# Clearing the zero tile first, modelling the last loads later, ranking the sink-row copies of V behind ready work, and a new order for TensorE

## The chip, the cores and the metric

The kernel runs on one core of a Trainium2 chip. The metric is the device time of one execution in microseconds (us), given as the median of the runs shown. The core's engines are named as in the profile: PE is TensorE (matrix products and transpositions), DVE is VectorE, ACT is ScalarE, POOL is GpSimd and SP is SyncE. POOL and SP also issue DMA transfers.

## The reference

Windowed attention with sinks over q, k and v of shape (4 batches, 8 heads, 768 rows, 64 wide), followed by a feed-forward block without a nonlinearity other than a product:

```python
scores = scale * np.matmul(q, k.transpose(0, 1, 3, 2))
keep = is_sink | in_window          # 4 sink keys, window of 128
a = softmax(np.where(keep, scores, -1e9))
x = np.matmul(a, v)                 # heads side by side: (3072, 512)
h = (x @ w1) * (x @ w2) @ w3        # 512 -> 1024 -> 1024
out = h @ w_out                     # 1024 -> 512
```

Inputs and output are float32; the kernel computes in bfloat16 with float32 sums.

## The kernel before

The work is cut into 350 TensorE tasks. Each task is a generator (a function with `yield` between its stages), and its later stages run on ACT, DVE or SP. The names in this text are the names of the tasks in the tables of the code:

- `("t3", i, h)`, function `fold_w3` (L525): four 128x128 transpositions of row block i of w3, half h, then a copy on DVE (L534). `("fm", i, h)`, function `fold_mm` (L548): two products of such a transposed block with w_out. Together they fold w3 and w_out into one matrix, w3o, which ACT copies out (L563, L566). The products of i = 4 to 7 keep one PSUM buffer from h = 0 to h = 3.
- `("tpk", b, kb)` (L244): eight transpositions of block kb of k and q of batch b, four of k first, then four of q, then one copy on DVE (L251). For batches 2 and 3 SP transposes by DMA instead (L256), one transfer for k and one for q of each block.
- `("sc", b, r, t)`: the score products of one unit, the exponential on ACT (L332, L385, L406), the mask product on DVE. `("ss", b, t)` is the same for the sink keys. `("av", ...)`: the products with V (L364, L435, L472) and the normalisation on DVE (a reciprocal and a product). `("xt", ...)` transposes the result on PE and copies it on ACT (L453, L492); for batches 1 to 3 SP does it by DMA (L499, `xd`).
- `("g", b, c, dt, half)`, function `gate` (L505): four products of the attention output with w1 (half 0, copied by ACT, L519) or w2 (half 1, multiplied by DVE, L516, into the tile `ab`). A gate has 256 columns in batches 0 and 1, and 320 (c = 0) or 448 (c = 1) in batches 2 and 3.
- `("p", b, m)`, function `project` (L569): eight products with w3o, a copy (L577), and the store to HBM (L582).
- `vo` (`own_values`, L272), for batches 2 and 3: DVE copies V rows into `vp` (L275), and then V's four sink rows into the blocks of `vN` that a unit reads (L278). `ko` (L259) copies keys into `kown` (L262 to L269).

PSUM has a pool of four buffers (`ps_mm`, for t3, tpk, av, xt, gates, projections, and fm of i = 4 to 7) and a pool of two (`ps_sc`, for scores and for fm of i = 0 to 3). A task takes the buffer that is oldest free, and so waits until ACT or DVE has emptied it.

The order is written by the program before it runs. `TURNS` (L827) is PE's list, task by task. `plan` (L903) walks through it with a table of durations and of arrival times of the loads (`landings`, L609, fills `arrive`), and gives ACT, DVE and SP their instructions in the order in which the model would start them. `LEAN` and `YIELD` are numbers that are added to a step's modelled start when two ready steps of one engine are compared: a higher one ranks the step later, a negative one earlier. Each engine executes its list strictly in this order, so an instruction that waits holds back everything behind it on its engine. Where the model sees a gap of over 0.5 us on PE in the first 40 us, `keep_busy` (L586) writes dummy products of a zero tile (`ksbd[1]`, the variable `idle`) into the list; their result, `pz`, is not read. How many there are follows from the modelled gap.

Loads go two ways. SP brings nine raw float32 blocks of w3 and w_out first (L181), and ACT and DVE cast them to bfloat16 (L539). SP's next instructions are eight little loads for `vc` (L225). When the fifth block is there, POOL starts its own loads, which convert on the way (L122 for k and q, L125 for V, L129 and L143 for weights), in the order of the list `order` (L165). With eight loads out, the next one waits for the oldest to land.

Of the kernel before, what the change touches and what calls it, by code (L numbers as in the profile page):

```python
# [21 lines left out]
def kernel(  # L22
# [13 lines left out]
    nc = tc.nc  # L36
# [68 lines left out]
    ksbd = [inp.tile([P, 648], BF16, name=f"ksbd_{b}") for b in range(2)]  # L105
# [59 lines left out]
    order = [("w3", 6, 8), ("qkv", 0, 0, 1), ("qkv", 0, 1, 2), ("w3", 5, 6), ("qkv", 0, 2, 3), ("qkv", 0, 3, 4),  # L165
# [23 lines left out]
    idle = ksbd[1][:, 0:512]  # L189
    nc.vector.memset(ident[:], 1.0)  # L190
    nc.vector.memset(maskt[:], 1.0)
    nc.vector.memset(vc[:], 0.0)
    for b in (1, 0):
        nc.vector.memset(ksbd[b][:], 0.0)  # L194
# [398 lines left out]
    arrive = {}  # L593
# [15 lines left out]
    def landings(RAW=2.0, POOL=3.0, DGE=1.3, RAMP=(0.75, 1.0)):  # L609
# [6 lines left out]
        while any(at[n] < len(q) for n, q in queues.items()):  # L616
# [11 lines left out]
            for n in busy:  # L628
                i = int(now - RAW) if now >= RAW else 0
                share = 1.0 if len(busy) == 1 else 0.5 if small not in "kqv" else 0.79 if n == "sp" else 0.13  # L630
                left[n][at[n]] -= 0.02 * share * (RAMP[i] if i < len(RAMP) else 1.0)
                if left[n][at[n]] <= 0.0:
                    lag, keys = queues[n][at[n]][2:]
                    for key in keys:
                        arrive[key] = now + lag + min(1.5, max(0.0, 0.25 * (now - 36.0))) + min(3.0, max(0.0, 0.1 * (now - 70.0)))
                    if n == "pool":
                        landed.append(now + lag)
                    at[n] += 1
# [158 lines left out]
    for b in range(B):  # L797
        for c, (t0, t1) in enumerate(CHUNKS[b]):
# [17 lines left out]
            for m in range(t0 // P, t1 // P):  # L816
# [10 lines left out]
    TURNS = [("t3", 0, 1), ("t3", 0, 0), ("t3", 2, 0), ("fm", 2, 0), ("t3", 4, 0), ("fm", 0, 0), ("t3", 2, 1), ("fm", 2, 1),  # L827
# [221 lines left out]
```

## Time and profile before

| what | us |
|---|---|
| median of 3 runs | 197.05 (196.99 to 197.65) |
| the profiled execution's own time | 196.85 |
| its span, first to last instruction | 195.1 |
| PE busy | 187.1 (96%) |
| DVE busy | 121.9 (62%) |
| ACT busy | 102.7 (53%) |
| POOL busy | 79.4 (41%) |

The profile comes from one execution. Its own time is 1.75 us longer than its span, which runs from the first to the last instruction. A row of the timeline has the start, the duration, the engine, the line of the code, the operation with output and input, and how many instructions were merged; in brackets stands how long the engine had been idle before and what ended that. Row names are without numbers, so `tp<-ident,w_sb` is a t3, `pz<-ksbd` a dummy, `ph` and `pw` are fm, `pg` a gate and `po` a projection. A group's row has the busy time and mean duration in ns, and after a second bar the idle time in front of it.

### The profile page before, as it was taken

Reading aid. Unit: us, or ns where it says so; the run is one execution under the profiler, and the core shown is the slowest. Engines: PE = TensorE matmul, PEld = TensorE weight load, DVE = VectorE, ACT = ScalarE, POOL = GpSimd, SP = SyncE. Lnnn points to the kernel's source line nnn. Section 1 sums busy time; section 2 is a strip of 40 time slices with the busy share of each in tenths; the row PEclk is TensorE's granted clock in tenths of the full one; section 3 lists DMA queues with packets and bytes.
Section 4 is the critical chain, followed back from the end, with each engine's and each line's share of the span. In section 5 each row is a group of like instructions: output and inputs, shape, how many; then the busy total and the mean of one; then the engine's idle time right before and its main releaser. Section 6 shows DMA issues by size and latency. Waiting matters only on the chain.

```text
span 195.1 us, 4747 instructions
## 1 busy us (share of the span) xinstructions
PE 187.1 (96%) x1880; PEld 123.7 (63%) x1880; DVE 121.9 (62%) x293; ACT 102.7 (53%) x172; POOL 79.4 (41%) x111
## 2 busy tenths in 40 slices
PE   3989999999999999999999999999899999999993
PEld 1444665898877776787986766665456665455542
DVE  4375689756789988778766686556567883124300
ACT  4051288753776768466446583365385653243322
POOL 5189977699999953532355343000000000000000
PEclk9999999999999999999999999999999999999999
DMA  6999999999999999999999999999930102420034
GB/s 218 370 388 174 169 160 199 194 161 154 157 152 182 188 128 125 156 186 192 116 184 151 127 200 148 216 187 131 208 72 0 35 16 79 133 108 0 0 105 168
DMA packets 110102, 29.43 MB, mean 151 GB/s; under 512 B 100736, under 2 KB 105984, under 8 KB 110080
## 3 DMA queue, kind: packets, MB, share of 16 engines
q0 software_dynamic: 81600, 12.59, 95.6%
q1 hardware_dynamic: 28336, 16.47, 40.2%
q8 instruction: 15, 0.25, 0.5%
q14 instruction: 7, 0.06, 0.1%
q10 hardware_dynamic: 144, 0.07, 0.1%
HBM read 29.90 MB, written 6.29 MB: 186 GB/s over the span
## 4 chain that ended last, share of the span: by engine, by line
PE 67%; DMA 28%; DVE 2%; issue 1%; POOL 0%; ACT 0%; POOLq 0%; DVEq 0%
PE pg L512 27%; DMA vN<-in_v_dram 17%; PE po L573 13%; DMA qN<-in_q_dram 10%; PE pw L559 4%; PE pz L590 3%; PE ph L559 3%; PE tp L249 3%; PE av L472 3%; PE sc L380 2%; PE tp L529 2%; PE av L435 1%; PE sc L402 1%; PE av L364 1%; PE sc L329 1%
## 5 line engine op out<-in xcount | busy, mean ns | idle before, releaser
L512 PE MATMUL pg<-xT,w_sb 128*128 128x256 bf16 (+2 forms) x640 | 92.0, 294 | 0.8 <-DVE ab L516 0.8
L512 PEld LDWEIGHTS <-w_sb 128*128 128x128 bf16 x640 | 59.8, 98 | 23.0 <-issue 1.9
L516 DVE TENSOR_TENSOR ab<-a_sb,pg 128x256 bf16<-128x256 f32 (+2 forms) x80 | 37.3, 472 | 32.7 <-PE pg L512 27.8
L519 ACT COPY a_sb<-pg 128x256 f32<-128x256 f32 (+2 forms) x80 | 32.8, 416 | 34.0 <-PE pg L512 28.9
L573 PE MATMUL po<-w3o,ab 128*128 128x512 bf16 (+2 forms) x208 | 44.4, 363 | 0.0
L573 PEld LDWEIGHTS <-ab 128*128 128x128 bf16 x208 | 19.3, 98 | 18.8 <-issue 0.2
L125 POOL DMA_DIRECT2D vN<-in_v_dram x26 | 23.5, 908 | 16.5 <-DMA kN<-in_k_dram 8.6
L577 ACT COPY w_sb<-po 128x512 f32<-128x512 f32 (+2 forms) x25 | 14.1, 564 | 28.0 <-PE po L573 27.8
L122 POOL DMA_DIRECT2D qN<-in_q_dram x24 | 21.7, 903 | 10.2 <-DMA vN<-in_v_dram 5.6
L332 ACT ACTIVATE ex<-sc 128x928 bf16<-128x928 f32 (+1 forms) x24 | 22.5, 972 | 4.5 <-PE sc L329 4.5
L122 POOL DMA_DIRECT2D kN<-in_k_dram x24 | 21.7, 906 | 7.2 <-DMA qN<-in_q_dram 3.2
L385 ACT ACTIVATE ex<-sc 128x1024 bf16<-128x1024 f32 (+1 forms) x16 | 15.1, 970 | 3.2 <-PE sc L380 3.0
L336 DVE TENSOR_TENSOR am<-ex,maskt 128x928 bf16<-128x928 bf16 (+1 forms) x24 | 15.3, 652 | 2.3 <-ACT ex L332 2.2
L371 DVE TENSOR_TENSOR xn<-av,rec 112x256 bf16<-112x256 f32 (+1 forms) x24 | 11.2, 468 | 0.8
L364 PEld LDWEIGHTS <-am 128*128 128x128 bf16 x208 | 8.9, 98 | 2.5
L590 PE MATMUL pz<-ksbd 128*128 128x512 bf16 x20 | 7.2, 521 | 3.2 <-DVE ksbd L194 3.2
L390 DVE TENSOR_TENSOR am<-ex,maskt 128x1024 bf16<-128x1024 bf16 (+1 forms) x16 | 10.0, 648 | 0.2 <-ACT ex L385 0.2
L251 DVE COPY kqT<-tp 128x1024 bf16<-128x1024 bf16 x12 | 8.3, 689 | 2.9 <-PE tp L249 2.8
L364 PE MATMUL av<-vN,am 128*128 128x65 bf16 x144 | 9.4, 193 | 0.0
L559 PE MATMUL ph<-wo_sb,kown 128*128 128x512 bf16 x32 | 9.1, 380 | 0.2
L534 DVE COPY kown<-tp 128x512 bf16<-128x512 bf16 x12 | 4.9, 420 | 6.7 <-PE tp L529 6.6
L406 ACT ACTIVATE ex<-sc 128x1024 bf16<-128x1024 f32 x7 | 7.1, 1029 | 3.7 <-PE sc L402 3.7
(85 smaller groups left out, 186.4 us busy)
## 6 DMA issues: line engine op xcount, KB each, us to landing
out_dram<-w_sb SPq DMA_DIRECT2D x20, 256.0 KB
vN<-in_v_dram POOLq DMA_DIRECT2D x26, 128.0 KB, 8.9
kN<-in_k_dram POOLq DMA_DIRECT2D x24, 128.0 KB, 8.0
qN<-in_q_dram POOLq DMA_DIRECT2D x24, 128.0 KB, 8.3
w_sb<-in_moe_w_dram POOLq DMA_DIRECT2D x9, 256.0 KB, 8.2
ab<-in_moe_w_dram SPq DMA_DIRECT2D x4, 512.0 KB
ab<-in_moe_w_out_dram SPq DMA_DIRECT2D x2, 512.0 KB
out_dram<-w_sb SPq DMA_DIRECT2D x7, 128.0 KB
```

Source lines behind the costliest of these rows:

```text
L122: nc.gpsimd.dma_start(out=heads(dst[b][:, kb, :]), in_=rows(src, b, kb * P, (kb + 1) * P))
L125: nc.gpsimd.dma_start(out=vN[b][:, s, :, 0:D], in_=rows(v, b, t0, t1))
L332: nc.scalar.activation(ex[:, :, 0:n], sc[:, :, 0:n], ACTF.Exp, scale=scale)
L336: nc.vector.tensor_mul(am[:, :, 0:n], ex[:, :, 0:n], maskt[:, mv:mv + 1, 0:n].to_broadcast([P, 2, n]))
L364: nc.tensor.matmul(o, lhs, rhs, start=(x == 0), stop=(x == len(todo) - 1), skip_group_check=True)
L385: nc.scalar.activation(ex[:, :, c0:], sc[:, :, c0:], ACTF.Exp, scale=scale)
L512: nc.tensor.matmul(pg[:], w_sb[:, kk, dt * P:(dt + 1) * P], xT[b][:, kk, tk], start=(kk == 0), stop=(kk == NP - 1))
L516: nc.vector.tensor_mul(ab[b][:, dt, tk], gate_a.pop((b, c, dt))[:], pg[:])
L519: nc.scalar.copy(a_sb[:], pg[:])
L559: nc.tensor.matmul(po, w3T[i][:, j, :], wo_sb[:, j, :], start=(j == 0), stop=(j == KFF - 1))
L573: nc.tensor.matmul(po[:], ab[b][:, kk, m * P:(m + 1) * P], w3o[:, kk, n0:n1], start=(kk == 0), stop=(kk == KFF - 1))
L577: (nc.vector.tensor_copy if n0 == DM // 2 else nc.scalar.copy)(o_sb, po[:])
```

## The change

Five things are changed.

1. In the program's head, the tile of zeros that the dummies read is the first that DVE clears. Before, it was the fourth (the identity, the masks and `vc` came first).
2. In POOL's list of loads, block 2 of batch 0 (k, q, v) goes ahead of row block 5 of w3.
3. In `landings`, loads that the model has landing after 112 us are taken to land up to 4.5 us later.
4. `YIELD` has an entry for `vo`, 0.8: a copy of V's rows ranks behind other work that would start up to 0.8 us after it.
5. `TURNS` and `LEAN` are replaced. The same 350 tasks stand in TURNS, in another order.

```diff
-    order = [("w3", 6, 8), ("qkv", 0, 0, 1), ("qkv", 0, 1, 2), ("w3", 5, 6), ("qkv", 0, 2, 3), ("qkv", 0, 3, 4),
+    order = [("w3", 6, 8), ("qkv", 0, 0, 1), ("qkv", 0, 1, 2), ("qkv", 0, 2, 3), ("w3", 5, 6), ("qkv", 0, 3, 4),
...
     idle = ksbd[1][:, 0:512]
+    nc.vector.memset(ksbd[1][:], 0.0)
     nc.vector.memset(ident[:], 1.0)
     nc.vector.memset(maskt[:], 1.0)
     nc.vector.memset(vc[:], 0.0)
-    for b in (1, 0):
-        nc.vector.memset(ksbd[b][:], 0.0)
+    nc.vector.memset(ksbd[0][:], 0.0)
...
-                        arrive[key] = now + lag + min(1.5, max(0.0, 0.25 * (now - 36.0))) + min(3.0, max(0.0, 0.1 * (now - 70.0)))
+                        arrive[key] = now + lag + min(1.5, max(0.0, 0.25 * (now - 36.0))) + min(3.0, max(0.0, 0.1 * (now - 70.0))) + min(4.5, max(0.0, 0.2 * (now - 112.0)))
...
-    TURNS = [("t3", 0, 1), ("t3", 0, 0), ("t3", 2, 0), ("fm", 2, 0), ("t3", 4, 0), ("fm", 0, 0), ("t3", 2, 1), ("fm", 2, 1),
+    TURNS = [("t3", 0, 0), ("t3", 4, 0), ("t3", 2, 0), ("fm", 0, 0), ("t3", 0, 1), ("fm", 4, 0), ("fm", 0, 1), ("t3", 4, 1),
...
-    LEAN = {(("t3", 2, 0), 1): -0.4, (("t3", 3, 0), 1): -1, (("sk", 0), 0): 0.4, (("xt", 0, 0, 1), 1): 1, (("sc", 0, 1, 2),
+    LEAN = {(("c", "wo", 2, 0), 0): 1, (("t3", 0, 1), 1): 1, (("t3", 5, 0), 1): -2.5, (("t3", 7, 0), 1): 1, (("tpk", 0, 2),
...
-    YIELD = {"g": 0.0, "av": 0.0, "sc": 0.4, "tdk": 1.5, "tdq": 1.5}
+    YIELD = {"vo": 0.8, "g": 0.0, "av": 0.0, "sc": 0.4, "tdk": 1.5, "tdq": 1.5}
```

What stands in the engines' lists now. On DVE at the start of the program, before (ksbd_1_112 is the zero tile; tp3_205 and tp3_210 are t3(0,1) and t3(0,0); tp3_225 is t3(2,0); ab_0_103 and ab_1_104 hold raw weights, the second cast is row block 2 of w3 and the third row block 4):

```order
L190 MEMSET ident_73 128x128
L191 MEMSET maskt_75 128x1536
L192 MEMSET vc_74 128x128
L194 MEMSET ksbd_1_112 128x324
L194 MEMSET ksbd_0_111 128x324
L539 CAST w3_sb_80<-ab_0_103 128x1024
L534 COPY kown_2_109<-tp3_205 128x512
L534 COPY kown_2_109<-tp3_210 128x512
L539 CAST w3_sb_80<-ab_0_103 128x1024
L534 COPY kown_3_110<-tp3_225 128x512
L539 CAST w3_sb_80<-ab_1_104 128x1024
```

The same place of the same engine in the changed kernel (tp3_205 is t3(0,0), tp3_227 is t3(4,0), tp3_232 is t3(2,0)):

```order
L190 MEMSET ksbd_1_112 128x324
L191 MEMSET ident_73 128x128
L192 MEMSET maskt_75 128x1536
L193 MEMSET vc_74 128x128
L194 MEMSET ksbd_0_111 128x324
L539 CAST w3_sb_80<-ab_0_103 128x1024
L534 COPY kown_2_109<-tp3_205 128x512
L539 CAST w3_sb_80<-ab_0_103 128x1024
L539 CAST w3_sb_80<-ab_1_104 128x1024
L534 COPY kN_1_88<-tp3_227 128x512
L534 COPY kown_3_110<-tp3_232 128x512
```

The zero tile has moved from the fourth place to the first, and the three casts of w3 have only one copy between them. PE's list begins with 12 dummies, t3(0,1), t3(0,0), 6 dummies, t3(2,0), 2 dummies before; now with 12 dummies, t3(0,0), 13 dummies, t3(4,0), t3(2,0), and no dummy after that.

On DVE late in the program, where the last V blocks of batch 3 are copied, before (vN_3_94 is V of batch 3; av_2530 and av_2560 are av(3,2,0) and av(3,3,0); pg_2550, pg_2589 and pg_2596 are the gates (2,1,0,1), (2,1,2,1) and (2,1,1,1)):

```order
L371 TENSOR_TENSOR xn_2495<-av_2530,rec_2547 128x3x128
L275 COPY vp_3_108<-vN_3_94 128x576
L278 COPY vN_3_94<-vN_3_94 4x1152
L516 TENSOR_TENSOR ab_2_105<-a_sb_2557,pg_2550 128x448
L269 COPY kown_3_110<-kqT_3_98 128x4x124 x2
L368 RECIPROCAL rec_2586<-av_2560 128x6
L371 TENSOR_TENSOR xn_2495<-av_2560,rec_2586 128x3x128
L516 TENSOR_TENSOR ab_2_105<-a_sb_2594,pg_2589 128x448
```

And there now (av_2538 and av_2567 are av(3,2,0) and av(3,3,0); pg_2560, pg_2588, pg_2604 and pg_2640 are the gates (2,1,0,1), (2,1,1,1), (2,1,2,1) and (2,1,3,1)):

```order
L371 TENSOR_TENSOR xn_2475<-av_2538,rec_2556 128x3x128
L516 TENSOR_TENSOR ab_2_105<-a_sb_2549,pg_2560 128x448
L368 RECIPROCAL rec_2585<-av_2567 128x6
L371 TENSOR_TENSOR xn_2475<-av_2567,rec_2585 128x3x128
L269 COPY kown_3_110<-kqT_3_98 128x4x124 x2
L516 TENSOR_TENSOR ab_2_105<-a_sb_2565,pg_2588 128x448
L516 TENSOR_TENSOR ab_2_105<-a_sb_2593,pg_2604 128x448
L275 COPY vp_3_108<-vN_3_94 128x576
L278 COPY vN_3_94<-vN_3_94 4x1152
L516 TENSOR_TENSOR ab_2_105<-a_sb_2609,pg_2640 128x448
```

The two copies of V have moved behind three gate products, the normalisation of av(3,3,0) and a copy of keys.

On SP at about the same time, before (kN_3_90 and qN_3_86 are k and q of batch 3, kqT_3_98 their transposes; xT_3_102 is the transposed attention output; the last kN and the last qN here are block 5):

```order
L256 DMA_TRANSPOSE kqT_3_98<-kN_3_90 128x4x128
L582 DMA out_0_dram<-w3_sb_80 128x512
L256 DMA_TRANSPOSE kqT_3_98<-qN_3_86 128x4x128
L582 DMA out_0_dram<-w3_sb_80 128x512
L499 DMA_TRANSPOSE xT_3_102<-xn_2495 128x4x128 x2
L499 DMA_TRANSPOSE xT_3_102<-xn_2495 128x4x64
L499 DMA_TRANSPOSE xT_3_102<-xn_2722 128x4x112 x2
```

And there now:

```order
L582 DMA out_0_dram<-w3_sb_80 128x512 x3
L256 DMA_TRANSPOSE kqT_3_98<-qN_3_86 128x4x128
L582 DMA out_0_dram<-w3_sb_80 128x512
L499 DMA_TRANSPOSE xT_3_102<-xn_2475 128x4x128 x2
L499 DMA_TRANSPOSE xT_3_102<-xn_2475 128x4x64
L256 DMA_TRANSPOSE kqT_3_98<-kN_3_90 128x4x128
L499 DMA_TRANSPOSE xT_3_102<-xn_2744 128x4x112 x2
```

Block 5's transposition of k has moved behind that of q and behind the three transfers of xT of unit (3,0).

More of the change, by code (lines that the diff above doesn't have):

```diff
@@ L824 @@
                          + [folded(i) for i in range(KFF)], ring="mm")
-    TURNS = [("t3", 0, 1), ("t3", 0, 0), ("t3", 2, 0), ("fm", 2, 0), ("t3", 4, 0), ("fm", 0, 0), ("t3", 2, 1), ("fm", 2, 1),
[54 rows of a table removed]
-    LEAN = {(("t3", 2, 0), 1): -0.4, (("t3", 3, 0), 1): -1, (("sk", 0), 0): 0.4, (("xt", 0, 0, 1), 1): 1, (("sc", 0, 1, 2),
-            1): 0.4, (("sc", 0, 1, 2), 2): -0.4, (("sc", 0, 3, 2), 2): 1, (("sk", 1), 0): 0.4, (("xd", 1, 0, 0), 0): -2.5,
-            (("xd", 1, 0, 1), 0): -0.4, (("sc", 1, 0, 2), 1): -2.5, (("tdk", 2, 0), 0): -1, (("tdk", 2, 1), 0): -1, (("tdq",
[7 rows of a table removed]
+    TURNS = [("t3", 0, 0), ("t3", 4, 0), ("t3", 2, 0), ("fm", 0, 0), ("t3", 0, 1), ("fm", 4, 0), ("fm", 0, 1), ("t3", 4, 1),
[54 rows of a table added]
+    LEAN = {(("c", "wo", 2, 0), 0): 1, (("t3", 0, 1), 1): 1, (("t3", 5, 0), 1): -2.5, (("t3", 7, 0), 1): 1, (("tpk", 0, 2),
[11 rows of a table added]
     HOP = 0.2
     MARGIN = {"av": 0.3}
-    YIELD = {"g": 0.0, "av": 0.0, "sc": 0.4, "tdk": 1.5, "tdq": 1.5}
+    YIELD = {"vo": 0.8, "g": 0.0, "av": 0.0, "sc": 0.4, "tdk": 1.5, "tdq": 1.5}
     PACE = [[0, 0, 0], [0, 0, 0], [0, 0, 7.6], [8.9, 3, 5.4]]
```

124 rows, old and new, of tables (LEAN, TURNS) are left out of this document.

## The prediction

> **What bounds the kernel now.** I read the page first, then who TensorE (PE) waited for, then its busy time in two long stretches. The columns of the waits are total, times and longest in us.
>
> ```profile
> span 195.1 us, 4747 instructions
> ```
>
> ```profile
> PE pz L590 <- DVE ksbd L194: 3.2, 1, 3.2
> PE pg L512 <- DVE ab L516: 0.8, 1, 0.8
> ```
>
> ```profile
> 15.73:139.02 123.29, 123.29 (x1419) 89.19 (x1418) 88.51 (x222) 74.25 (x126) 71.01 (x89) 1.00 1.93 165
> 140.02:191.80 51.78, 51.77 (x400) 29.30 (x399) 23.72 (x54) 22.64 (x39) 0.00 (x0) 1.00 0.22 64
> ```
>
> In the second fence a stretch is followed by its length and by PE's busy time: PE has no gap in 123.29 us and none in 51.77 us. It waits at the start and once at 139 us. Both kernels give it the same 350 tasks, so the end moves only with those gaps, with the dummies (pz) among useful work, and with the few changes of matmul shape. The start and the place around 139 us therefore carry the argument. Here is the start, from the timeline (start, duration, then instruction):
>
> ```profile
> 0.91 0.17 DVE L190 MEMSET ident<- 128x128 bf16 x1 [0.91 <-PEq L1030]
> 2.83 0.67 DVE L194 MEMSET ksbd<- 128x324 uint32 x2
> 3.22 5.10 PE L590 MATMUL pz<-ksbd 128*128 128x512 bf16 x12 [3.22 <-DVE ksbd L194]
> 8.15 0.61 PE L529 MATMUL tp<-ident,w_sb 128*128 128x128 bf16 x8
> 8.60 1.46 PE L590 MATMUL pz<-ksbd 128*128 128x512 bf16 x6
> 9.12 0.25 SPq L225 DMA_DIRECT2D vc<-in_v_dram  x1
> 9.25 0.68 DVE L539 CAST w_sb<-ab 128x1024 bf16<-128x1024 f32 x1
> 10.23 0.59 PE L590 MATMUL pz<-ksbd 128*128 128x512 bf16 x2
> 10.91 0.61 PE L559 MATMUL ph<-wo_sb,kown 128*128 128x512 bf16 x2
> 11.98 0.40 PE L529 MATMUL tp<-ident,w_sb 128*128 128x128 bf16 x4 [0.46 <-DVE w_sb L539]
> ...
> 14.61 1.29 PE L559 MATMUL ph<-wo_sb,kown 128*128 128x512 bf16 x4
> 15.73 0.39 PE L529 MATMUL tp<-ident,w_sb 128*128 128x128 bf16 x4
> ...
> 30.82 0.40 PE L249 MATMUL tp<-ident,kN 128*128 128x128 bf16 x4
> ```
>
> A PE row's duration laps 0.17 over the next (14.61 + 1.29 = 15.90, yet 15.73 starts), so starts count. The first 12 dummies step by about 0.42 (5.10 / 12), the later ones by about 0.22 ((1.46 - 0.17) / 6). The fast step is there from 8.15 on, 4.9 us after the first dummy. From the start of useful work (8.15) to tpk(0,3), the fourth q/k transposition of batch 0 (30.82), 22.67 us pass. Of these 8 dummies take 8 x 0.22 = 1.76, and three waits 1.1: 10.91 - 10.23 - 2 x 0.22 = 0.24, 11.98 - 10.91 - 2 x 0.22 = 0.63, and 15.73 - 14.61 - 4 x 0.22 = 0.24. That leaves 19.8 us of useful work ahead of tpk(0,3).
>
> **The zero tile first.** Two clears of ksbd take 0.67, so one takes 0.33. DVE starts at 0.91, so the first dummy can start at about 1.3 instead of 3.22. The list has 12 dummies, one weight transposition, 13 dummies (25, before 20). With the fast step 4.9 us after the first, the 12 end at 6.4, the 13 at about 9.5. Then t3(4,0) must have its cast: SP's little loads each start when a weight load has landed, and 9.12 stands for the third. One cast of 0.69 behind that gives 9.85, so t3(4,0) starts at 9.9. ident and the masks come 0.33 later; ident is first needed at 6.4, so nothing shows it.
>
> A rule speaks against a fixed count: the Trainium skill ("TensorE: Matmul & The Clock Gate", Part 1) says that the warm-up is a time, a free-running window of about 3.4 us, so that the number of slow matmuls differs from run to run. This trace's 4.9 us fits one to two such windows, though its granted clock reads 1.00 throughout. An estimate by the page, opening between 3.4 and 6.8 us after the first, would end the dummies between 8.8 and 10.3 instead of 9.5; the sum would be the same, as the next paragraph's bound lies later.
>
> **The front, up to tpk(0,3).** Order of the tasks: behind tpk(0,3) there now stand t3(5,0), av(0,2,0), fm(7,3), fm(5,0) and xt(0,0,0); ahead of it now stands t3(5,1). The chain has the first group in one piece and the last alone:
>
> ```profile
> 28.98 0.22 PE tp L529 x4
> 29.21 0.24 PE av L435 x8
> 29.45 0.88 PE pw L559 x4
> 30.33 0.22 PE xt L451 x4
> ...
> 31.77 0.33 PE tp L529 x4
> ```
>
> So 1.56 goes behind it and 0.22 comes ahead: 1.34 less to do. 19.8 - 1.34 = 18.5, of which t3(0,0) is done early, so 18.2 are left from 9.9: without a wait PE would reach tpk(0,3) at 28.1. But its q block is not there:
>
> ```profile
> L122 POOL DMA_DIRECT2D qN<-in_q_dram x1: 873/873/873, 22.4 to 22.4; - x1
> DMA to landing us min/median/max: 7.1/7.1/7.1
> ```
>
> It lands at 22.35 + 7.1 = 29.45. The swap of w3's row 5 with block 2 leaves as many loads ahead of it, so I keep that. Its four q transposes stand 0.22 behind the four of k, so tpk(0,3) starts at 29.3. Every other wait on the way (a cast, an earlier q block, w3's row 5 now loaded later) is free as long as they come to less than 29.3 - 28.1 = 1.2. Gain there: 30.82 - 29.3 = **1.5**. Given back behind it: 1.34 of moved work, less two changes between narrow score matmuls and the others (56 now, 58 before; 0.1 each, as 31.77 shows 0.33 where 28.98 shows 0.22): **1.1**.
>
> **The copy of V's sink rows.** Around 139 us:
>
> ```profile
> 136.60 0.30 DVE L275 COPY vp<-vN 128x576 bf16<-128x576 bf16 x1
> 137.51 1.68 PE L512 MATMUL pg<-xT,w_sb 128*128 128x448 bf16 x8
> 138.99 0.45 DVE L278 COPY vN<-vN 4x1152 bf16<-4x1152 bf16 x1 [2.09 <-DMA vN<-in_v_dram]
> 139.36 0.60 DVE L516 TENSOR_TENSOR ab<-a_sb,pg 128x448 bf16<-128x448 f32 x1
> 140.02 1.67 PE L512 MATMUL pg<-xT,w_sb 128*128 128x448 bf16 x8 [0.83 <-DVE ab L516]
> ```
>
> ```profile
> L125 POOL DMA_DIRECT2D vN<-in_v_dram x1: 873/873/873, 121.5 to 121.5; - x1
> DMA to landing us min/median/max: 17.4/17.4/17.4
> ```
>
> DVE stands 2.09 us before the last V block's landing (121.5 + 17.4 = 138.9); the gate product behind it frees a PSUM buffer for PE, which loses 0.83 + 0.17 = 1.0. In the changed order three gate products and the normalisation of av(3,3,0) stand ahead of this copy: its neighbour g(2,1,2,1) runs on PE at 140.02 - 1.4 + 2 x 0.76 (two gates moved ahead) = 140.1, and its product ends on DVE at 141.5. The copy is reached 2.6 us after the landing: **1.0** goes. Behind it then stand g(2,1,3,1)'s product and two masks, and the next thing that can be late is the landing itself, if it comes after 141.5. The later modelled loads have no instruction of their own; they act only through this order.
>
> **The sum.** -1.5 + 1.1 - 1.0 = -1.4. For new short waits in the crowded stretch from 29 to 37 us I add 0.2, between 0 (none seen there before) and 1.0 (one exponential, below). The profiled execution has 196.85 us for a span of 195.1; behind PE's last result (191.83 before) both orders end alike, on ACT's copy and the last store:
>
> ```profile
> 191.83 0.27 ACT w_sb L577
> ```
>
> So 196.85 - 1.2 = 195.65; the median of the runs, 197.05, lies 0.2 above the profiled one, which gives **195.8**. Changes under 0.5% (1.0 us) count as none, about what a measurement of this kernel can tell.
>
> **Rivals.**
>
> *A, a new wait between 20 and 37 us.* fm(6) and fm(7) now hold two of the four PSUM buffers together from about 24 to 27 us (before one after the other), and xt(0,2,0) and g(0,0,1,0) follow closely on DVE copies and on ACT exponentials:
>
> ```profile
> L332 ACT ACTIVATE ex<-sc 128x928 bf16<-128x928 f32 (+1 forms) x24 | 22.5, 972 | 4.5 <-PE sc L329 4.5
> ```
>
> One exponential too late costs up to 1.0: 196.1 to 196.8, say 196.4. For it: in the 6.2 us of PE work from sc(0,0,1) to g(0,0,1,0) ACT has three exponentials (2.9) and four copies in a row, each on a chain to a task in that stretch. Against: what falls before 29.3 is free.
>
> *B, the late V landing moves too,* past 141.5, as transposes and stores come 0.4 to 1.4 us sooner and share the engines with it: the old 1.0 stays, 196.8. Against: the same bytes, and 2.6 us of room.
>
> *C, a cold front.* If the fast step never comes in the dummies, 25 x 0.42 = 10.5 us end at 11.9 plus the transposes, 2.1 later than 9.9; 1.2 of it is free, 0.9 costs: 196.7. By the rule of the skill above it could not come that late.
>
> *D, the slower side: SyncE's queue.* In the new order the last q block's transposition stands first, then three of xT, and the last k block's behind all (before: k, q, xT).
>
> ```profile
> 135.58 1.19 SPq L256 DMA_TRANSPOSE kqT<-kN  x1
> 137.83 1.19 SPq L256 DMA_TRANSPOSE kqT<-qN  x1
> 139.11 0.53 SPq L582 DMA_DIRECT2D out_dram<-w_sb  x1
> 139.89 0.47 DVE L269 COPY kown<-kqT 128x496 bf16<-128x496 bf16 x2
> 141.12 4.42 SPq L499 DMA_TRANSPOSE xT<-xn  x3
> ...
> 150.16 0.22 PE L329 MATMUL sc<-kqT 64*128 64x112 bf16 x2
> ```
>
> q at 137.83, the store, 4.42 for xT: k's transposition starts at about 144.0. It had landed 139.89 - 135.58 = 4.3 after its issue at the latest, which gives 148.3, the kown copy 148.8; the scores that need it stand at 150.16 - 1.4 + 1.3 (a gate of 448 and one of 320 columns moved ahead, 0.76 and by width 0.54) = 150.1. There is 1.3 of room. If the last q block lands 1.3 us later, each further us costs one; slower than before by 1.0 needs 1.3 + 1.4 + 1.0 = 3.7 us, a landing at 141.5. At 142 it gives 198.5. For it: loads that took 7.1 us early take 17.4 there. Against: order and bytes of the loads are the same, and 4.3 is an upper bound. The Trainium skill ("DMA: Bandwidth & Descriptors", Issuing engines are not separate DMA queues) says that all issuers share the same 16 engines; no run here has the late queue alone.
>
> *E, the front is freer:* if that q block lands 0.8 earlier, PE can follow (its own work would let it come 1.2 earlier): 195.0. Nothing in the change aims at this load; only its neighbours move.
>
> **How the numbers follow.** Forecast 0.57 (its own range 195.4 to 196.05), A 0.21, B 0.06, C 0.04, D 0.07, E 0.05. Faster by over 0.5%, under 196.06: forecast and E, 0.62. Within: A, B, C, 0.31. Slower: 0.07. From 194.9 (E's end) to 196.9 (A, B, C) leaves out D and little else.
>
> **What the changed profile would show.** The first dummy at 1.3; t3(4,0) near 9.9; tpk(0,3)'s q transposes at 29.5; no PE gap over 0.3 after that; no wait of L278 for a DMA; PE's end near 190.6. I am wrong if PE waits between 30 and 190, if DVE waits for vN, or if tpk(0,3) starts after 30.

## The result and the profile after

The changed kernel takes 195.72 us (median of 6 runs, 195.42 to 196.27), the kernel before 196.92 beside it (6 runs): a ratio of 0.9938 with a 95% interval of 0.9916 to 0.9961. The forecast was 195.8. Two later groups with the changed kernel unaltered (below) gave 195.96 and 195.98, so the time itself is steady, while the kernel before moved from 196.31 to 196.93 between the later groups, and the ratios there were 1.0003 and 0.9982. The ratios leave out executions over 1.5% above a kernel's fastest, and the kernel before, which scatters more (194.3 to 199.6), loses more of them (9 of 35 in the group with 1.0003, the changed kernel none); medians in the text are those of all runs.

The page and the waits of TensorE (PE) in the profiled execution of the changed kernel (195.84 us); the columns of the waits are total, times and longest in us:

```profile
span 194.0 us, 4745 instructions
```

```profile
PE pz L590 <- DVE ksbd L190: 1.3, 1, 1.3
PE pw L559 <- DVE kown L534: 0.8, 1, 0.8
PE tp L529 <- DVE w_sb L539: 0.4, 1, 0.4
```

The wait of a gate for DVE at 139 us is gone, the first wait is 1.9 shorter, and a new one is there: fm(6,0) (`pw`) waits for a copy on DVE. The timeline shows where it comes from, and how the place at 139 us looks now:

```profile
1.33 5.02 PE L590 MATMUL pz<-ksbd 128*128 128x512 bf16 x12 [1.33 <-DVE ksbd L190]
6.42 2.97 PE L590 MATMUL pz<-ksbd 128*128 128x512 bf16 x13
9.81 0.62 PE L529 MATMUL tp<-ident,w_sb 128*128 128x128 bf16 x8 [0.42 <-DVE w_sb L539]
...
20.73 0.69 DVE L291 TENSOR_TENSOR vs<-vc,ones_s 128x512 bf16<-128x512 f32 x1 [2.69 <-DMA vc<-in_v_dram]
21.34 0.42 DVE L534 COPY kown<-tp 128x512 bf16<-128x512 bf16 x1
21.82 0.60 PE L559 MATMUL pw<-wo_sb,kown 128*128 128x512 bf16 x2 [0.77 <-DVE kown L534]
...
29.53 0.39 PE L249 MATMUL tp<-ident,kN 128*128 128x128 bf16 x4
...
141.54 0.62 DVE L516 TENSOR_TENSOR ab<-a_sb,pg 128x448 bf16<-128x448 f32 x1 [0.89 <-PE pg L512]
142.08 0.30 DVE L275 COPY vp<-vN 128x576 bf16<-128x576 bf16 x1
142.42 0.45 DVE L278 COPY vN<-vN 4x1152 bf16<-4x1152 bf16 x1
```

The first dummy, the end of the dummies and t3(4,0) stand where the forecast had them. At 18 us DVE has run out of ready work and stands 2.69 us before its product for `vc` (L291, which needs all eight little loads), and the copy that fm(6,0) needs is queued behind it. In the kernel before, DVE came to the same product when its data were there:

```profile
21.16 0.68 DVE L291 TENSOR_TENSOR vs<-vc,ones_s 128x512 bf16<-128x512 f32 x1
```

In the changed kernel, tpk(0,3) starts at 29.53 (forecast 29.3). At 142.42 DVE comes to the copy of V's sink rows and does not wait; that block's landing was at 121.90 + 14.4 = 136.3. Behind tpk(0,3) PE is busy without a break but for a gap of 0.1 that ends at 62.1. Two stretches show it (length of the stretch, then PE's busy time); in the 4.39 us between them PE is busy throughout as well:

```profile
29.53:138.25 108.72, 108.61 (x1280) 80.55 (x1279) 79.12 (x202) 67.85 (x119) 58.81 (x74) 1.00 1.94 166
142.64:190.56 47.92, 47.92 (x372) 27.42 (x368) 21.54 (x49) 21.50 (x38) 0.00 (x0) 1.00 0.21 63
```

PE's last product starts at 190.56, before at 191.57: 1.01 earlier, as the spans (194.0 and 195.1) and the times of the two profiled executions (195.84 and 196.85) are.

### The profile page after: what moved, and what is told of

Same layout as the page of the kernel before. It is cut to its first block, busy times and chain, and to the rows that moved or that the text cites. A ratio compares the mean times of both kernels' runs of the same rounds, so it can differ in the third digit from the quotient of the medians.

```text
span 194.0 us, 4745 instructions
## 1 busy us (share of the span) xinstructions
PE 187.9 (97%) x1885; PEld 124.1 (64%) x1885; DVE 120.8 (62%) x293; ACT 102.6 (53%) x172; POOL 79.6 (41%) x111
## 4 chain that ended last, share of the span: by engine, by line
PE 86%; DMA 8%; SPq 2%; DVE 1%; issue 1%; ACT 0%; DVEq 0%
PE pg L512 44%; PE po L573 21%; DMA kqT<-in_moe_w_dram 6%; PE av L364 3%; PE sc L329 3%; PE pw L559 3%; DMA vc<-in_v_dram 3%; PE av L472 3%; PE tp L249 2%; PE sc L380 2%; SPq L181 2%; PE sc L402 1%; PE av L435 1%; PE ph L559 1%; PE xt L451 0%
## 5 line engine op out<-in xcount | busy, mean ns | idle before, releaser
L512 PEld LDWEIGHTS <-w_sb 128*128 128x128 bf16 x640 | 59.5, 98 | 22.3 <-issue 1.2
L122 POOL DMA_DIRECT2D qN<-in_q_dram x24 | 22.2, 926 | 16.0 <-DMA kN<-in_k_dram 7.0
L122 POOL DMA_DIRECT2D kN<-in_k_dram x24 | 22.2, 923 | 8.1 <-DMA qN<-in_q_dram 2.9
L332 ACT ACTIVATE ex<-sc 128x928 bf16<-128x928 f32 (+1 forms) x24 | 22.7, 973 | 3.4 <-PE sc L329 3.0
L590 PE MATMUL pz<-ksbd 128*128 128x512 bf16 x25 | 8.0, 487 | 1.3 <-DVE ksbd L190 1.3
L368 DVE RECIPROCAL rec<-av 112x4 f32<-112x4 f32 (+1 forms) x24 | 4.4, 184 | 7.7 <-PE av L364 7.3
```

The costliest lines, as they stand in the source:

```text
L122: nc.gpsimd.dma_start(out=heads(dst[b][:, kb, :]), in_=rows(src, b, kb * P, (kb + 1) * P))
L332: nc.scalar.activation(ex[:, :, 0:n], sc[:, :, 0:n], ACTF.Exp, scale=scale)
L512: nc.tensor.matmul(pg[:], w_sb[:, kk, dt * P:(dt + 1) * P], xT[b][:, kk, tk], start=(kk == 0), stop=(kk == NP - 1))
```

## The experiments

Two numbers place every run: when tpk(0,3) starts (the end of the front), and when PE's last product starts. The runs with an edit and the two repeats had 10 to 12 executions each, the changed kernel's first comparison 6; the ratio is to the kernel before in the same group. Most edits change numbers from which the program writes the lists, so the order of instructions in the traces says what an edit moved. The two runs with vc modelled later differ from the changed kernel in the place of L291 alone, the copy alone and both small edits differ from the kernel before in what their names say. The runs with the landing model back, q block 3 sooner and t3(6,0) later move some other instructions of DVE too, the first two also block 5's transposition of k on SP.

| run | median us | ratio, 95% interval | tpk(0,3) | last product |
|---|---|---|---|---|
| before, its first profile | 197.05 | | 30.82 | 191.57 |
| changed, first profile | 195.72 | 0.9938 (0.9916 to 0.9961) | 29.53 | 190.56 |
| zero tile fourth again | 195.85 | 0.9996 (0.9967 to 1.0025) | 29.67 | 190.51 |
| landing model back | 196.19 | 0.9994 (0.9968 to 1.0019) | 29.75 | 191.00 |
| vc modelled later | 195.24 | 0.9957 (0.9924 to 0.9990) | 28.65 | 189.91 |
| q block 3 sooner | 195.85 | 0.9993 (0.9967 to 1.0018) | 29.41 | 190.88 |
| changed again | 195.96 | 1.0003 (0.9976 to 1.0030) | 29.70 | 190.87 |
| before + copy moved | 195.31 | 0.9955 (0.9918 to 0.9993) | 30.04 | 189.80 |
| changed + 7 dummies | 195.98 | 0.9980 (0.9946 to 1.0013) | 29.03 | 189.96 |
| before + zero first | 196.11 | 0.9997 (0.9959 to 1.0035) | 30.00 | 190.88 |
| before + zero + copy | 194.94 | 0.9937 (0.9909 to 0.9965) | 29.85 | 189.69 |
| the same, t3(6,0) later | 194.45 | 0.9912 (0.9885 to 0.9940) | 28.99 | 188.75 |
| changed, third time | 195.98 | 0.9982 (0.9957 to 1.0008) | 29.71 | 190.46 |
| vc later, again | 195.26 | 0.9940 (0.9917 to 0.9962) | 28.51 | 189.49 |

The kernel before had 196.31, 196.93 and 196.56 in the three groups of four.

### The zero tile fourth again

```diff
-    nc.vector.memset(ksbd[1][:], 0.0)
     nc.vector.memset(ident[:], 1.0)
     nc.vector.memset(maskt[:], 1.0)
     nc.vector.memset(vc[:], 0.0)
-    nc.vector.memset(ksbd[0][:], 0.0)
+    for b in (1, 0):
+        nc.vector.memset(ksbd[b][:], 0.0)
```

> The changed kernel, but with the zero tile cleared fourth again, as before; everything else stays. The first dummy then starts at about 3.2 instead of 1.33, the 25 dummies end about 1.4 later (9.0 to 10.4 plus the step of the slow ones), and t3(4,0) starts near 11.2 instead of 9.81. Theory (the front ends at a load): three later waits of the changed kernel end at times that the start does not set, 0.29 at 11.1 (a cast), 0.28 at 19.7 (q block 0, landed 19.95) and 0.93 at 20.8 (DVE behind the little loads for vc). They take up 1.5, so tpk(0,3) still starts at 29.5 to 29.6 and the time is the changed kernel's or up to 0.2 more: 195.7 to 195.9. Rival (the front is one chain from the zero tile on): the 1.4 goes straight through, tpk(0,3) at 30.9, 197.1.

195.85, with tpk(0,3) at 29.67: the theory's number. But its cause was not put to the test, because the start was not 1.4 late. From the timeline:

```profile
3.22 4.12 PE L590 MATMUL pz<-ksbd 128*128 128x512 bf16 x12 [3.22 <-DVE ksbd L194]
7.18 0.39 PE L529 MATMUL tp<-ident,w_sb 128*128 128x128 bf16 x4
7.40 2.97 PE L590 MATMUL pz<-ksbd 128*128 128x512 bf16 x13
10.21 0.61 PE L529 MATMUL tp<-ident,w_sb 128*128 128x128 bf16 x8
...
20.88 0.69 DVE L291 TENSOR_TENSOR vs<-vc,ones_s 128x512 bf16<-128x512 f32 x1 [2.52 <-DMA vc<-in_v_dram]
...
29.67 0.39 PE L249 MATMUL tp<-ident,kN 128*128 128x128 bf16 x4
```

The first dummy is at 3.22 as wanted, but the 12 dummies take 4.12 instead of 5.02: the fast step came about 2.7 us after the first dummy, not 4.9. So t3(4,0) was only 0.4 late. tpk(0,3) was 0.14 later than in the first profile, which is what vc's product was later (20.88 against 20.73). The run with more dummies has a later t3(4,0).

### The landing model back

```diff
-... + min(3.0, max(0.0, 0.1 * (now - 70.0))) + min(4.5, max(0.0, 0.2 * (now - 112.0)))
+... + min(3.0, max(0.0, 0.1 * (now - 70.0)))
```

> The changed kernel, but with the term for loads after 112 us taken out of the model again; PE's list and the rank of vo stay. DVE's list then has the last copy of V's sink rows ahead of the reciprocal of av(3,2,0): it would be reached at about 135.2 instead of 142.4. Theory (the order of DVE's list took the stall away): DVE stands until the last V block lands. With the landing of the kernel before, 138.9, it stands 3.7, and the four gates' and attention's buffers behind it stop PE for 1 to 2: 196.7 to 197.7. Rival (the landing came sooner by itself, 136.32 in the changed kernel, and would have removed the stall in any order): DVE stands about 1.1 and PE loses 0 to 0.3: 195.7 to 196.0.

196.19, between the two. The timeline of this run:

```profile
137.47 0.45 DVE L278 COPY vN<-vN 4x1152 bf16<-4x1152 bf16 x1 [2.03 <-DMA vN<-in_v_dram]
...
138.67 2.63 PE L512 MATMUL pg<-xT,w_sb 128*128 128x448 bf16 x13 [0.27 <-DVE xn L371]
```

V landed at 137.4, DVE stood 2.03, and PE lost 0.4. So without the later model DVE's list does wait again, and the order is what avoids it; but the price follows the landing, which came neither at 138.9 nor at 136.3. The last product is 0.44 later than in the changed kernel's profile: 0.22 from the front, and 0.22 behind it, which is this wait's 0.4 less the gap at 62.1, which this execution doesn't have. The time alone shows no difference from the changed kernel (0.9994 here, 0.9982 and 1.0003 there).

### vc modelled later

```diff
-    arrive["vc",] = 20.0
+    arrive["vc",] = 21.5
```

> The changed kernel, but with the model's arrival of vc at 21.5 instead of 20.0, so that DVE copies the transposed weights of t3(7,0) and t3(6,0) and the first q/k block ahead of the product that waits for vc. The wait of 0.93 in front of fm(6,0) goes. Theory (the front ends at the landing of q block 3): tpk(0,3) can come no sooner than 29.23, since its q half needs the landing at 29.45; it starts at 29.53 in the changed kernel, so at most 0.3 is won: 195.4 to 195.7. Rival (PE's own work and waits set the front): all 0.9 is won, tpk(0,3) at 28.6, 194.8.

195.24, last product 0.65 earlier, tpk(0,3) 0.88 earlier:

```profile
20.55 0.69 DVE L251 COPY kqT<-tp 128x1024 bf16<-128x1024 bf16 x1 [0.15 <-PE tp L249]
21.16 0.68 DVE L291 TENSOR_TENSOR vs<-vc,ones_s 128x512 bf16<-128x512 f32 x1
...
28.65 0.39 PE L249 MATMUL tp<-ident,kN 128*128 128x128 bf16 x4
```

DVE does the copies first and no longer waits at L291. The start of tpk(0,3) is the rival's (28.6); the median lies between the theory's 195.4 to 195.7 and the rival's 194.8. q block 3 landed at 28.76 here, 0.7 sooner than in the first profile, so it allowed 28.54, 0.1 ahead of tpk(0,3), and this run alone does not tell whether it would have been the bound. The repeats below do.

### q block 3 sooner

```diff
-... ("qkv", 0, 2, 3), ("w3", 5, 6), ("qkv", 0, 3, 4),
+... ("qkv", 0, 2, 3), ("qkv", 0, 3, 4), ("w3", 5, 6),
...
-    arrive["vc",] = 20.0
+    arrive["vc",] = 21.5
```

(and t3(5,1) behind t3(5,0) in PE's list)

> As the kernel with vc modelled at 21.5, and block 3 of batch 0 (k, q, v) loaded ahead of row block 5 of w3 as well, with t3(5,1) moved behind t3(5,0) in PE's list since its rows now land later. Theory (q block 3 sets the end of the front): q block 3 lands about 1.2 sooner, at 28.2; PE, without the 0.93 and with t3(5,1) moved behind, can be at tpk(0,3) at 28.3; 1.2 is won there, and 0.22 given back for t3(5,1): about 1.0 less than the changed kernel, 194.7, if no new wait appears up to 37 us. Rival (another resource takes over, ACT's exponentials or the weight loads behind): 195.4 to 195.7, with a PE wait between 29 and 37.

195.85: 0.15 above the rival's range, with a PE wait between 29 and 37 as the rival had it, but one of 0.24 only. It is 0.61 more than with the vc edit alone, though the executions of the two overlap. q block 3 came at 28.65, within the 28.4 to 29.45 that it had in the other runs of the changed order, so the swap did not move it by the 1.2 expected. What PE met instead were the earlier q blocks:

```profile
20.19 0.40 PE L249 MATMUL tp<-ident,qN 128*128 128x128 bf16 x4 [0.57 <-DMA qN<-in_q_dram]
...
23.79 0.40 PE L249 MATMUL tp<-ident,qN 128*128 128x128 bf16 x4 [0.39 <-DMA qN<-in_q_dram]
...
31.94 0.38 PE L529 MATMUL tp<-ident,w_sb 128*128 128x128 bf16 x4 [0.24 <-ACT w3o L563]
```

Why q block 1 landed at 23.75 here and in the first profile, and at 22.7 to 23.2 in the seven other runs with the same loads ahead of it, is open.

### The changed kernel again

> The changed kernel once more, unaltered, so that the others of this group have it beside them on the same chip. The profiles so far have shown that loads land up to 1 us apart from one execution to the next in the first 30 us and up to 2.8 at 136 to 139, and that the fast step of the dummies begins 2.6 to 4.9 us after the first. If the gain of the change is as steady as the first comparison gave it, 0.9938 of the kernel before; if a good part of it hung on such an execution of the kernel before (late fast step, V at 138.9), 0.996 to 0.999.

195.96 against 196.93 of the kernel before in the medians, a ratio of 1.0003 (0.9976 to 1.0030). By the ratio it is the second case and a little beyond it; the medians of all runs give 0.9951, between the two cases. The time is the forecast one; the distance to the kernel before is smaller than in the first comparison. In its profile:

```profile
20.90 0.69 DVE L291 TENSOR_TENSOR vs<-vc,ones_s 128x512 bf16<-128x512 f32 x1 [2.60 <-DMA vc<-in_v_dram]
...
21.99 0.61 PE L559 MATMUL pw<-wo_sb,kown 128*128 128x512 bf16 x2 [0.90 <-DVE kown L534]
...
29.70 0.39 PE L249 MATMUL tp<-ident,kN 128*128 128x128 bf16 x4
```

q block 3 landed at 28.78 here and would have allowed 28.56. PE was 1.1 later, 8.80 behind L291 as in the other profiles with this order.

### The copy alone

```diff
-    LEAN = {(("t3", 2, 0), 1): -0.4, ...
+    LEAN = {(("vo", 3, 2), 1): 0.8, (("t3", 2, 0), 1): -0.4, ...
```

in the kernel before; it moves one instruction of DVE and nothing else.

> The kernel before with one instruction of DVE moved: the last copy of V's sink rows stands four products, two masks' worth of work and two kown copies later, as in the changed order; all other lists are the same. DVE then reaches it near 141.5 and does not wait. Theory (the stall hangs on the landing): the kernel before reaches the copy at 136.9 and PE loses what the landing is later than about 137.9, 1.0 in its profile (138.9) but nothing with the landings of four of the five other profiles (136.1 to 137.4) and 0.2 with 138.1. The median then gains 0 to 0.4. Rival (the stall is there in every execution): the median gains 1.0, 0.995 of the kernel before.

195.31, ratio 0.9955 (0.9918 to 0.9993): the rival's number. V landed at 138.66 in this execution, and nothing waited:

```profile
141.24 0.64 DVE L336 TENSOR_TENSOR am<-ex,maskt 128x928 bf16<-128x928 bf16 x1 [0.43 <-ACT ex L332]
141.80 0.44 DVE L278 COPY vN<-vN 4x1152 bf16<-4x1152 bf16 x1
```

With PE's old list, V landed at 138.9, 138.7, 138.2, 137.2 and 135.2 in five profiles; with the new one at 136.0 to 138.1 in nine. My reading, that four of five executions have no stall, took landings under the new list for those under the old; of the five, three are past the 137.9 from which PE loses time. One moved copy gains more than the whole change did in this group (195.96).

### Seven dummies more

```diff
-keep_busy(int((gap - 0.25) / (0.22 if start > 9.0 else 0.43)))
+keep_busy(int((gap - 0.25) / (0.22 if start > 9.0 else 0.43)) + 7 * (start > 9.0))
```

> The changed kernel with 20 instead of 13 dummies behind t3(0,0). Seven more are 1.5 us; 0.4 to 0.7 of it falls into PE's wait for the cast in front of t3(4,0), which then starts 0.8 to 1.1 later, at about 10.9. Theory (the later waits end at loads and casts): the waits of 0.3 at 11.1, 0.3 to 0.6 at 19.8 and 0.65 to 0.93 at 20.8 take it up; tpk(0,3) at 29.5 to 29.9 and 0 to 0.2 more time. Rival (a chain of PE's own work): 0.8 to 1.1 more, tpk(0,3) at 30.4 to 30.6.

195.98, the same as the changed kernel in its group (195.96):

```profile
6.58 4.48 PE L590 MATMUL pz<-ksbd 128*128 128x512 bf16 x20
10.90 0.61 PE L529 MATMUL tp<-ident,w_sb 128*128 128x128 bf16 x8
...
20.13 0.69 DVE L291 TENSOR_TENSOR vs<-vc,ones_s 128x512 bf16<-128x512 f32 x1 [1.28 <-DMA vc<-in_v_dram]
...
29.03 0.39 PE L249 MATMUL tp<-ident,kN 128*128 128x128 bf16 x4
```

t3(4,0) is 1.1 later than in the first profile and tpk(0,3) 0.5 earlier, below the theory's 29.5. In this execution vc landed 0.6 earlier (20.13), and from t3(4,0) on PE waits for nothing: 29.03 - 10.90 = 18.13 us of work in one piece. So here no load set tpk(0,3), but PE's own work behind a late start. The later start cost nothing because it only took up waits that were there otherwise, as the theory has it; with these loads a still later one would have passed through. One of the 12 executions took 507.53 us; nothing here shows why.

### The zero tile first, alone

The kernel before with the `memset` of `ksbd[1]` ahead of `ident`'s.

> The kernel before with the zero tile cleared first and nothing else changed. First dummy at 1.33, the 12 end by 5.3 to 6.4, t3(0,1) at 6.2 behind its cast. Theory (loads and casts bound the front): t3(4,0) can start at 9.85 (w3's third block) instead of 11.98, and tpk(0,3) not before q block 3, 29.2; nothing is moved behind it, so all that it wins stays: 0.9 to 1.5 against the profile of the kernel before (30.82), less against executions in which the fast step begins early, 0.2 to 0.9 in the median. Rival one (the start does not matter because casts hold everything): 0 to 0.1. Rival two (the start passes straight through): 1.9.

196.11, ratio 0.9997 (0.9959 to 1.0035): rival one by the ratio, though the interval leaves room for the lower part of the theory's range, and the medians of all runs are 0.82 apart, which is inside it. The profile says more: tpk(0,3) at 30.00, as with the zero tile fourth in the run above (30.04). It shows the two waits that go with PE's old list:

```profile
18.58 0.40 PE L529 MATMUL tp<-ident,w_sb 128*128 128x128 bf16 x4 [0.51 <-DMA w_sb<-in_moe_w_dram]
...
30.00 0.40 PE L249 MATMUL tp<-ident,kN 128*128 128x128 bf16 x4
...
138.30 0.45 DVE L278 COPY vN<-vN 4x1152 bf16<-4x1152 bf16 x1 [2.22 <-DMA vN<-in_v_dram]
...
139.33 1.68 PE L512 MATMUL pg<-xT,w_sb 128*128 128x448 bf16 x8 [0.96 <-DVE ab L516]
```

t3(6,0) waits for w3's rows 6 and 7, POOL's first load, and tpk(0,3) follows 11.4 later (30.00 here; in the run with the copy alone, with the zero tile fourth, 18.61 and 30.04). The first profile of the kernel before has the same 11.4, but no wait:

```profile
19.41 0.39 PE L529 MATMUL tp<-ident,w_sb 128*128 128x128 bf16 x4
```

There the fast step of the dummies had come late, and PE was behind the load, so that tpk(0,3) stood at 30.82. The 12 dummies took over 5 us in only 3 of the 14 profiles, and the three other profiles with PE's old list unaltered have tpk(0,3) at 29.85 to 30.04. So the 30.82 from which my gain was counted was probably a late one; the kernel before as it stands has no second profile.

### Both small edits

> The kernel before with two small edits: the zero tile cleared first, and the last copy of V's sink rows moved behind (as in the run with the copy alone). PE's list, the loads and the rest stay as before. Theory (PE's new list costs, because it waits for vc; the copy is what gains): the same time as the copy alone, since w3's rows 6 and 7 (landing near 18.5) end PE's first stretch in either case: PE's last product starts near 189.7, median 195.1 to 195.4, and less than the unaltered changed kernel of this group by 0.4 to 0.8. Rival (the new list gains and the two edits only get it started): 195.9 to 196.5, slower than the changed kernel.

194.94, ratio 0.9937 (0.9909 to 0.9965), 0.2 under the range of the theory, and 1.04 less than the changed kernel in the same group (195.98), more than the 0.4 to 0.8 expected. PE's last product is at 189.69, as forecast, although its front lost 0.4 once more, to q block 2 at 27.19:

```profile
17.98 0.40 PE L529 MATMUL tp<-ident,w_sb 128*128 128x128 bf16 x4 [0.63 <-DMA w_sb<-in_moe_w_dram]
...
27.19 0.40 PE L249 MATMUL tp<-ident,qN 128*128 128x128 bf16 x4 [0.28 <-DMA qN<-in_q_dram]
...
29.85 0.40 PE L249 MATMUL tp<-ident,kN 128*128 128x128 bf16 x4
```

The theory holds: with PE's old list, one `memset` moved and one copy moved, the kernel is faster than with the new list.

### t3(6,0) later

```diff
-("fm", 2, 3), ("t3", 6, 0), ("fm", 1, 3), ("t3", 3, 0), ("t3", 6, 1),
+("fm", 2, 3), ("fm", 1, 3), ("t3", 3, 0), ("t3", 6, 0), ("t3", 6, 1),
```

on top of both small edits; the number for the last copy is 1.6 here, because with 0.8 the program would have put it back ahead of the products.

> As the run with both small edits, and t3(6,0) moved two places later in PE's list, behind fm(1,3) and t3(3,0) (0.66 of ready work). PE's wait of 0.56 to 0.68 for w3's rows 6 and 7 should go. Theory (that landing bounds the front of this list): all of it is won, tpk(0,3) at 29.3 to 29.4 instead of 30.0, PE's last product at 189.1 to 189.3, median 194.6 to 194.9. Rival (vc, landing at 20.7 to 20.9, is next in line): DVE's product for vc now stands 0.6 sooner and waits, behind it the copy that fm(3,0) needs, and half or more is lost again: 195.0 to 195.3.

194.45, ratio 0.9912 (0.9885 to 0.9940), the fastest of all: 1.5 less than the changed kernel beside it. Its timeline:

```profile
17.58 1.06 PE L529 MATMUL tp<-ident,w_sb 128*128 128x128 bf16 x16
18.81 0.60 PE L559 MATMUL pw<-wo_sb,kown 128*128 128x512 bf16 x2 [0.18 <-DVE kown L534]
...
20.10 0.69 DVE L291 TENSOR_TENSOR vs<-vc,ones_s 128x512 bf16<-128x512 f32 x1 [1.01 <-DMA vc<-in_v_dram]
...
28.99 0.40 PE L249 MATMUL tp<-ident,kN 128*128 128x128 bf16 x4
```

The wait for w3's rows is gone, 16 transpositions run in one piece. DVE now waits 1.01 for vc, as the rival said, but nothing that PE needs stands behind it for long. In this execution w3's rows 6 and 7 landed at 17.0, 0.9 to 1.5 sooner than in the other runs with the old list, so part of the 28.99 is that. The median gains 0.49 on the run without this edit, as the theory had it, but the two overlap too much to call that clear of noise (193.91 to 195.71 here, 194.50 to 195.61 in ten of the 12 executions there).

### The changed kernel a third time, and vc later beside it

> The changed kernel, unaltered, for comparison within this group. Theory (its front hangs on the landing of vc): tpk(0,3) starts 8.8 after DVE's product for vc (8.80, 8.79, 8.80, 8.80 in four profiles with that order of DVE, with vc from 20.73 to 20.95), whatever the dummies and q block 3 do; PE's last product 161.0 to 161.3 after tpk(0,3). Rival (q block 3): tpk(0,3) starts 0.22 ahead of that block's landing, whatever vc does.

> The changed kernel with vc modelled at 21.5, again, beside the unaltered changed kernel. Theory (the wait for vc is what the new list costs): 0.6 to 1.0 less than the changed kernel of this group, PE's last product near 189.9 as with the copy alone. Rival (the 195.24 of the first such run was that group's chip or its loads): within 0.3 of the changed kernel.

195.98 and 195.26: 0.72 apart, as in the theory, ratios 0.9982 (0.9957 to 1.0008) and 0.9940 (0.9917 to 0.9962). The timeline of the unaltered kernel, and the landing of q block 3 in it (the answer covers k and q of that block; 6.9 is q's):

```profile
20.91 0.69 DVE L291 TENSOR_TENSOR vs<-vc,ones_s 128x512 bf16<-128x512 f32 x1 [2.45 <-DMA vc<-in_v_dram]
...
29.71 0.39 PE L249 MATMUL tp<-ident,kN 128*128 128x128 bf16 x4
```

```profile
L122 POOL DMA_DIRECT2D qN<-in_q_dram x1: 873/873/873, 22.2 to 22.2; - x1
DMA to landing us min/median/max: 6.9/7.0/7.1
```

8.80 from vc's product to tpk(0,3), for the fifth time. q block 3 landed at 29.14 and allowed 28.92, so it was not the bound. PE's last product came 160.75 after tpk(0,3), 0.25 under the range I had given (the gap at 62.1 is not there in this execution). With vc later, DVE does not wait at L291, and tpk(0,3) is 1.2 earlier (q block 3, landed at 28.39, allowed 28.17 there):

```profile
28.51 0.39 PE L249 MATMUL tp<-ident,kN 128*128 128x128 bf16 x4
```

## Why the prediction was right, and where it was not

The time was right (195.8; 195.72, 195.96 and 195.98 measured), two of the three large terms were right, and the third, the front, came out nearly right by luck.

**The start: right.** First dummy 1.33 (1.3), dummies' end 6.42 + 2.97 - 0.17 = 9.2 (9.5), t3(4,0) 9.81 (9.9).

**The front: the number nearly right, the bound wrong.** The failed step is "Every other wait on the way ... is free as long as they come to less than 29.3 - 28.1 = 1.2." PE's own work was right: I had 18.2 from t3(4,0) to tpk(0,3), and the run with seven more dummies has 18.13 without a wait. In the first profile it is 29.53 - 9.81 = 19.7, so the waits came to 1.6: 0.29 at 11.4 (a cast), 0.28 at 19.7 (q block 0), 0.93 at 20.9 and about 0.1 at 22.3 (DVE, behind vc). What I took for the bound, q block 3, landed at 29.45 exactly as forecast, and that luck hid the error there (29.53 against 29.3). In four other profiles with this order it landed 0.3 to 0.7 sooner, and tpk(0,3) stood at 29.67 to 29.75 all the same. In all five tpk(0,3) starts 8.80 behind DVE's product for vc, so the landing of vc was the bound; with that product ranked later, in two runs, tpk(0,3) starts at 28.65 and 28.51. I had seen DVE's lists at this place and did not ask what DVE waits for there: in the old order vc's product found its data at 21.16 without a wait, in the new one DVE came to it at 18 with PE's copies behind it. Rival A named a new wait between 20 and 37 us, but looked for it in PSUM buffers and exponentials, and let everything before 29.3 count as free.

**What is given back: right.** I had 1.1, and 0.2 for new waits. From tpk(0,3) to the last product it is 190.56 - 29.53 = 161.03 in the changed kernel and 189.80 - 30.04 = 159.76 with the old list and no stall: 1.27, of it about 0.3 the gap at 62.1 (the third run of the changed kernel, without it, has 160.75).

**The copy of V's sink rows: right.** With the old list and the stall it is 191.57 - 30.82 = 160.75 (and 190.88 - 30.00 = 160.88): the stall costs 160.75 - 159.76 = 1.0 (and 1.1). The changed DVE list reaches the copy at 142.42, where I had 141.5. That the landing itself came 2.6 sooner (136.3) was not expected; in the run with the landing model back, where DVE comes to this copy early, it waited 2.03 for a landing at 137.4, so the order is still needed.

**The sum, and what it stands on.** In the two profiled executions: -1.29 - 0.99 + 1.27 = -1.01, against my -1.4 + 0.2 = -1.2. But two of the terms depend on the execution. Against the 30.0 that the other profiles with PE's old list have, the front gains 0.3, and the sum is 0 even with a stall of 1.0, which three of five landings gave. This fits the ratios of 0.9982 and 1.0003 in the later groups, but it is not shown to be their cause: by the medians of all runs the changed kernel is still 0.58 and 0.97 us faster there, and the kernel before has one profile only. So the forecast time stands, while the distance to the kernel before, 1.2 in the first comparison, is not as steady as the sum made it. I had added 0.2 for the median of the runs over the profiled execution, and had no way to see from one profile that its start was a late one.

**The rivals.** B (V lands past 141.5), D (SyncE's queue, 198.5) and C (a cold front) did not happen: kown's last copy ran at 148.21 directly behind other work of DVE. E was the nearest to an opportunity: the front can be freer by 0.9 to 1.2, but through vc, not q block 3.

**Which part gains.** One instruction of DVE moved in the old list gives 195.31, with the zero tile moved as well 194.94, the whole change with its new list 195.98 beside it. The new list costs what the copy gains, by the wait for vc: with vc modelled 1.5 later it comes to 195.26. The lowest median, 194.45, keeps PE's old list and removes its wait for w3's rows by moving one task two places; against the changed kernel (195.98) that is clear, against the two small edits alone (194.94) it is not.

## What to carry to other kernels

When a searched order moves an engine's work ahead, look on every in-order engine for the instruction in the crowded stretch that waits for a load, and ask what is queued behind it: here a product that nobody needed for 13 us (its first reader, av(0,0,1), runs at 34.2) held back a copy that PE needed at once. A bound that fits one profile to 0.2 us need not be the bound; the sign is that it moves from one execution to the next and the end does not move with it. Try the smallest edit that removes a wait by itself before a new list: it can be worth more than the list that contains it.

## What the runs showed of the hardware

The start of the fast step of the dummies differs from one execution to the next, with the same instructions ahead. The 12 dummies took 5.10 and 5.02 in the first two profiles, and 4.07 to 5.30 in the 12 others; of the 12 between 6 and all are slow (a step of 0.43, then 0.22), so that the step changes 2.5 to about 5.6 us after the first. The granted clock in the rows reads 1.00 all the while. The Trainium skill ("TensorE: Matmul & The Clock Gate", Part 1) says that the window is free-running and that the count of slow products differs from run to run; this agrees. My estimate of 3.4 to 6.8 us from that page was too late for 8 of the 14 profiles; the measured 2.5 to 5.6 decide.

Loads of the same bytes in the same order land up to 1.7 us apart in the first 30 us (q block 0, with the same loads ahead in all 14 profiles, at 18.8 to 20.5; q block 1 at 22.7 to 23.8 with the changed order), and the last V block at 135.2 to 138.9 with 14 to 18 us from issue to landing. An order that brings DVE to that copy at 135 to 137 leaves it to chance whether PE waits; one that comes to it at 140.8 to 142.7 did not wait in any of the eleven profiles that had it.
